# A hand-ordered attention and MLP kernel, with the order of all its tasks and loads written anew

## The chip, the cores and the metric

The kernel runs on one core of a Trainium2 chip. A core has a matrix engine (TensorE; in the profile PE, its weight loads PEld), a vector engine (VectorE, DVE), a scalar engine (ScalarE, ACT), a general engine (GpSimd, POOL) and SyncE (SP), which here only issues DMAs. Each engine works through its own instructions strictly in order and waits on semaphores for the others. The metric is the device time of one execution in microseconds.

## The reference, cut to what matters

Block-sparse attention over 4 batches, 8 heads, 768 positions and 64 columns a head, and behind it a mixing block with weights 768 x 768, 512 x 2048 and 2048 x 512:

```python
scores = q @ k.T / 8                     # per batch and head
mask = near blocks | first/last block row and column | 3 sampled blocks per block row
x = softmax(where(mask, scores, -1e9)) @ v
tok = einsum('ts,bsd->btd', w_tok, alpha1 * x + beta1)
u = x + lam * tok
out = u + lam * (relu((alpha2 * u + beta2) @ w_ch1) @ w_ch2)
```

## The kernel before, in words

The kernel has a fixed prologue and then one long list of words, `ORDER`. A loop reads the list from its first word to its last, and each word emits one task. Since every engine works in order, the list fixes the order of the tasks on each engine; a word also names a PSUM bank (`q0:0`) or an engine (`hq1:d` is VectorE, `:a` ScalarE) where there is a choice. Nothing else schedules the work.

Heads go in 16 pairs p (four a batch). The words, in the order in which a pair needs them:

- `lq`, `lk`, `lv` p: GpSimd issues the load of a pair's q, k or v. Six tiles take turns for these, so a load waits until an earlier tile has been cast. `lt`, `lc`, `lw`, `lx` load the weights and vectors in the same way.
- `cq`, `ck`, `cv` p: a cast or copy of what was loaded, on ScalarE or VectorE. `cq0` is the second head of the first pair, whose data come with the prologue.
- `H` h: TensorE transposes a head of the first five pairs; `hq` and `hk` copy the halves into the operands `qx` and `kx` (four of each, taken in turn). From the sixth pair on a DMA transposes (`tq`, `tk`).
- `hm0` copies the mask rows of `qx[0]` to `qx[1]`. Rows 64 to 87 of `qx` and `kx` carry the block mask in the first five pairs, so a score matmul reads them too. For `qx[2]` and `qx[3]` the prologue copies them by DMA on SyncE (line 401).
- `q` n: the scores of unit n (nine units of 1024 columns a pair), into two PSUM banks; `e` n: the exponential on ScalarE; `m` n: the mask on VectorE, from the sixth pair on; `p`, `r` n: scores times values; `n`, `nt`: the division.
- `M0` makes from the mask rows of `qx[3]` the mask for the later pairs, on VectorE; `N0` and `O0` send it through memory by DMA.
- `W`, `w`: the transposes of the token weights and their copies; `a`, `b`, `k`, `x`, `u`, `U`, `v`: the token mixing and the transposes behind it.
- `f`, `g`: the first channel matmul of batches 0 and 1 and its eviction with ReLU (`g` of the first 16 also copies a column `b1t`). For batches 2 and 3 `y` is a pair of matmuls in a scheme with seven products for eight, `d` its eviction (on ScalarE into a snapshot, or an addition on VectorE), `D` the ReLU. `P`, `S`, `T`, `V`, `Y`, `A` prepare operands on VectorE.
- `h`, `o`: the second channel matmul and its additions; `s`: the store.
- `z480`: a filler, a matmul of 480 columns that no one reads. `F`: a one-element write by VectorE behind which a later load is held.

The lines that the text speaks of:

```python
    for j in range(2, NQB):
        nc.sync.dma_start(qx[j][MB, :], qx[0][MB, :])          # lines 400, 401
    @on("M")
    def _(_i):
        nc.vector.tensor_scalar(
            out=rows[MB, :], in0=qx[3][MB, :], scalar1=-1.0, scalar2=F16MAX, op0=ALU.is_ge, op1=ALU.mult
        )                                                      # line 532
    for word in ORDER.split():
        ...
        step[kind](int(n), *args)
```

Of the kernel before, what the change touches and what calls it, by code (L numbers as in the profile page):

```python
# [54 lines left out]
ck3:d q25:1 F22 w0:d lk5 p12 w5:d e25 p13 q19:3 n2 W4:4 e19 H6:0 F28 lx3 w4:d q22:1 hk6:d r13:1
q17:2 e22 L1 q20:3 hq6:d e17 q24:1 L0 r14 H7:0 e20 q18:2 ck4:d a0 lv3 r15 e18 r16 r17 lc5 b0 q23:3
e24 cv2:d k1:4 n3 lk6 e23 lx1 q21:1 cq4:d r22:1 F42 x1 H9:5 e21 lv6 q28:3 F38 a1 p18:4 lw0 e28 r23
F40 q26:1 b1 p19 e26 hk9:d p20 r24 p21 hq7:d r25 cq6:a q27:3 cv4:d hq9:d r26 lq7 e27 p22 q30:1 hk7:d
k0:5 lw3 n5 e30 lc4 L2 H8:0 F23 F32 x0 q35:3 lw1 hk8:a hq8:d q31:1 lw2 k3:5 n4 e35 lx2 cv3:d q29:0
ck5:a x3 lq5 q32:3 ck6:d e31 k2:4 lk7 a2 e29 lx0 b2 p27:5 q34:1 x2 lv7 p28 u0:d e34 p29 p30 u3:d p31  # L60
lq8 r31:4 q33:0 e32 F37 n6 k4:2 e33 q39:3 x4 r32 u2:a F29 r33 e39 r34 r35 q37:0 n7 q38:1 U1:5 F25
ah6 e38 q40:3 ah7 k5:4 cv6:d e37 bh7 lk8 bh6 q36:1 cq7:d e40 x5 k7:0 lv5 F33 u4:d e36 B0 k6:1 x7
u1:a M0 p36:0 v1:a F39 u5:d p37 p38 x6 q41:1 u6:d U0:1 e41 q43:2 u7:d U2:6 S6 p39 e43 U3:7 v0:d
q44:1 v2:a v3:d p40 q42:2 F26 S7 r40:1 r41 e44 f0:6 f6:7 e42 f3:2 g0:a f5:3 cq5:d g3:d f1:6 tq5 lq11
g5:a F31 n8 r42 f8:2 N0 r43 g8:d f17:0 tk5 f24:3 r44 g24:d f9:2 tk6 S1 f11:3 g9:a g1:d f15:4 ck7:a
S4 f25:2 g11:a n9 f19:5 F30 S3 f12:1 S2 f2:3 g12:a S0 f31:6 g19:a S5 g15:a f26:1 T0 g2:a f10:4 f4:3
g10:a T1 f28:5 g26:a f20:4 g31:a T2 g25:a f16:1 ck8:a f7:2 a4 g4:a f23:6 g17:a T3 O0 f13:3 g7:a tq7
g28:a f18:0 cq8:d cv5:d g13:a f22:5 cv7:d tq6 g16:d g6:a f21:2 g23:d g22:a f27:1 g18:a tk8 P3:d
g20:a g21:d f14:3 g27:a P2:d f29:2 tk7 g14:a F34 b4 lk11 f30:0 g29:d lk9 tq8 cq11:d q53:2 g30:a
q48:1 P4:d k9:1 e53 lk12 A8 A0 lv8 e48 q50:3 q46:2 x9 h0:0 lq10 e46 A9 A1 h14:1 e50 A4 q52:1 o0  # L70
q49:2 e52 q45:3 A2 h1 A10 e49 h2 o12 A11 e45 h15 m48 P0:a F27 m50 lq9 q51:1 q47:2 m49 p48:6 e47 k8:7
F43 m45 m46 e51 p49 p50 o1 q58:2 x8 q56:1 e58 nt16 h16 m51 e56 m52 q60:2 q59:3 h3 o13 e60 A3 p45:2
m58 e59 p46 h17 m53 u8:a m47 u9:a q57:2 q55:3 F36 o2 e57 p47 U4 o14 p51:3 m59 h4 ck11:a m56 p52 e55
p53 nt15 lk14 q63:2 nt17 h18 e63 o3 q64:1 m57 q54:3 e64 q71:2 m60 h5 o15 e54 p57:2 a5 p58 h6 e71 b5
p59 ck12:a m64 q70:2 q62:3 nt19 e70 h19 lk10 m71 e62 q69:1 m54 q61:2 h20 F47 A5 ck9:a m55 p54:6
cq9:a k11:7 lv11 o16 e61 o4 tq9 lq13 h7:1 x11 cq10:a m62 k10:0 tk9 e69 m61 lv9 p60:7 A6 q67:2 tq10
m69 p55 e67 p56 o6 q80:1 x10 p61 e80 p62 nt18 q66:2 h8 nt20 e66 m70 q78:1 ck10:a q68:3 a6 p69:0 e68
p70 lk13 h9 m66 b6 e78 p71 o7 q65:2 q76:3 m63 u10:a q75:1 e65 nt23 h10 m67 u11:a p63:0 cv8:d k12:4
e76 m65 U5 lq12 m68 p66:5 e75 p64 x12 p67 tk10 p68 o8 q81:3 nt22 q86:1 e81 p65 h11 nt21 e86 m75
q74:2 q73:3 a7 e74 k13:0 b7 e73 q72:1 x13 q77:2 o9 u12:a k14:0 u13:a m76 e72 U6 k15:6 x14 A7 e77  # L80
p75:0 p76 x15 q79:1 u14:a m72 q85:2 u15:a h12 m77 e79 U7 m73 p77 e85 q82:3 m80 q93:1 s5 h13 m78 e93
tq11 m79 p78:4 p72:5 m74 e82 p73 p79 tk11 o10 p80 p74 q84:1 P1:d q87:3 nt24 e84 s0 f37:1 m86 tk12
f35:5 e87 nt26 f39:2 ck13:d g35:a m84 lq14 f54:3 g37:a nt25 g39:a q89:2 cv9:d q95:3 e89 q94:0 g54:d
lv10 f38:2 m82 e95 f32:3 P5:d P7:d f34:4 g32:a P6:d f48:5 e94 ck14:d m85 lk15 p84:3 a8 g34:a q83:3
q98:0 e83 p85 cq12:d f47:4 F44 F41 cv11:d tq12 lv15 m81 e98 p86 f61:6 g47:d lv12 g48:a p81:7 m83
q92:0 g61:a q88:2 b8 g38:a p82 f49:6 nt28 e92 m98 f36:2 e88 g49:d f63:3 m89 g36:a q106:0 m87 q91:2
g63:a p83 f51:6 e106 nt27 f56:2 m88 g51:a p87:3 cq13:d e91 f41:7 V0 m94 p88 g56:a q90:0 q96:2 cv10:d
g41:a m93 f52:2 e90 m92 p89 f57:6 m95 g52:a f53:7 e96 V2 p93:2 nt29 g57:a q97:0 q99:2 cq14:d e97
f33:3 m96 tq14 m91 p94 e99 p95 k16:6 m97 tk13 g33:a nt31 g53:a q104:0 m90 q102:1 s2 e104 q103:2 x16
f62:7 s1 a9 e102 tq13 p90:6 p91 p96:0 m99 p92 g62:a p97 nt30 tk14 p98 e103 f60:1 nt32 q113:1 m104  # L90
g60:a q100:2 s3 q105:3 e113 m102 s4 f59:0 b9 k17:1 e100 m113 F45 m103 lq15 e105 f55:2 x17 f44:3 lv14
g59:a m100 g55:a q108:2 m106 q107:0 lv13 e108 q101:3 m105 k18:2 a10 e107 p102:4 f50:5 m108 e101 x18
p99:0 p100 b10 g50:a f58:1 m101 g44:a p103 g58:a q131:3 m107 q115:1 p105:5 A20 e115 f45:1 A12 p106
e131 p104 A16 p101 p107 nt33 g45:a q112:1 k21:6 nt34 e112 nt35 q116:0 A21 q111:1 e116 q130:2 a11
k19:7 e111 x21 h35:0 x19 e130 m111 f43:1 m131 k20:2 g43:a A17 cv12:a o30 q109:2 V4 q114:3 e109 f40:1
A22 f42:3 m112 g40:a f46:4 e114 x20 m109 p111:1 h36 g46:a m114 g42:a cq15:d q110:2 m116 q133:1 e110
q126:3 b11 h37 m115 u16:a p112 ck15:a p113 p114:4 nt37 p115 e126 p116 tk15 p108:5 m130 p109 h28:1
e133 o31 A13 tq15 h38 cv14:a nt38 o24 u20:a q129:1 m110 q127:3 h29 A18 e127 A23 p110 e129 h30 nt36
o32 u21:a q134:2 A19 q132:1 e134 q128:3 o25 h39 m126 u17:a m129 q117:2 e128 U8 h31 m133 u18:a o33
p129:6 u19:a p130 m128 p131 e117 U9 k23:7 a12 e132 h40 o26 U10 nt43 cv15:a h41 x23 b12 u23:a q138:1  # L100
m127 q118:2 q119:3 e118 o34 h32 V5 cv13:a h21:0 m132 e119 m134 k25:4 o27 e138 k24:5 A14 x25 q142:1
o18 q143:3 A15 p126:4 p127 e143 x24 h33 m118 e142 p132:5 m117 h34 m138 p133 o28 p134 q141:1 nt44
q139:3 e141 p117:1 m143 p128 p118 h22 e139 nt42 m119 q135:1 a14 q125:2 e135 k22:6 b14 u24:a p119
e125 x22 h23 m141 u22:a q120:1 nt39 q140:2 e120 q137:3 U11 m142 k29:1 o19 e140 V1 k28:2 m125 u25:a
x29 e137 p141:3 U12 p142 m120 p143 h24 u29:a m139 m140 q123:2 q121:3 o20 e123 p138:1 x28 p139 h25
# [6 lines left out]
d125 p123:0 D124:a p124 a15 D132:a p125 y156 d135:a y163 b15 d147:a y155:1 y148:3 nt41 d142:a y149
d158 y137 y145:0 d151 d148:a k31:1 d145 d162:a V7 d155:a y144 a13 y138:3 d136:a y150 d143:a y157
d138 y164 y146 b13 d149:a y152:2 x31 D158:a y139 D137:d k26:5 u31:a d146 D144:a D145:d d152 d156:a
y159:0 d139 k27:1 d163:a D165:d D151:a x26 D123:a y166:3 x27 y151 y153 d166 u27:a k30:1 D138:d u26:a
d153 D166:a U13 d159 y167 D139:a D125:d y165 D152:a d167 y160 h42:5 D118:d D167:a D131:d d160 D153:a
# [962 lines left out]
```

## Time and profile before

| | us |
|---|---|
| median of three runs | 292.22 (292.13 to 292.43) |
| the profiled execution | 291.82 |
| its span, first to last instruction | 290.1 |
| TensorE busy | 283.9 |
| VectorE busy | 263.8 |
| ScalarE busy | 234.0 |
| GpSimd busy | 53.3 |

The span is the profile's time axis: every start in a row is counted from its first instruction. The profiled execution's own time is 1.7 us longer than its span. A row of a timeline gives start, length, engine, line and operation, output and inputs, how many instructions were merged into it and, in brackets, how long the engine had stood idle before and for whom it waited.

### The profile page before, as it was taken

The numbers are of one execution on the slowest core, as the hardware profiler recorded it, in microseconds if no ns is written. First come the engines' busy times: TensorE is split into PE (matmuls) and PEld (weight loads), VectorE is DVE, ScalarE is ACT, GpSimd is POOL, SyncE is SP. The second block draws the span as 40 slices with busy tenths as digits, with TensorE's granted clock in tenths as the row PEclk, the third lists the DMA queues.
The fourth block names the chain that finished last, engine by engine and source line by source line (L and its number), as shares of the span: only waits on it lengthen the run. The fifth ranks groups of instructions, "written<-read, shape, count | busy, mean of one in ns | idle before, by whom it ended". The sixth has DMA issues, their size and how long they took to land.

```text
span 290.1 us, 8529 instructions
## 1 busy us (share of the span) xinstructions
PE 283.9 (98%) x3538; PEld 213.6 (74%) x3538; DVE 263.8 (91%) x595; ACT 234.0 (81%) x350; POOL 53.3 (18%) x102
## 2 busy tenths in 40 slices
PE   8899999999999999999999999999999999999995
...
GB/s 161 189 246 210 195 211 194 203 165 176 168 115 30 53 140 118 74 164 135 27 186 146 7 2 57 85 3 47 37 75 0 19 112 0 148 145 1 2 42 177
DMA packets 47927, 30.95 MB, mean 107 GB/s; under 512 B 28792, under 2 KB 43984, under 8 KB 47888
## 3 DMA queue, kind: packets, MB, share of 16 engines
...
q14 instruction: 11, 0.09, 0.1%
HBM read 31.16 MB, written 6.88 MB: 131 GB/s over the span
## 4 chain that ended last, share of the span: by engine, by line
PE 87%; ACT 5%; DMA 4%; DVE 2%; issue 1%; POOL 0%; ACTq 0%
PE psum L907 26%; PE psum L997 13%; PE psum L828 12%; PE psum L661 11%; PE psum L763 11%; PE psum L634 9%; PE psum L624 4%; DMA wtk<-in_moe_w_tok_dram 3%; ACT hts L842 2%; ACT eT L645 2%; DMA k2f<-in_k_dram 1%; PE psum L806 1%; PE psum L355 1%; DVE a1p L733 0%; ACT rel L419 0%
## 5 line engine op out<-in xcount | busy, mean ns | idle before, releaser
L645 ACT ACTIVATE eT<-psum 128x1024 f16<-128x1024 f32 (+1 forms) x145 | 140.4, 1028 | 9.3 <-PE psum L634 5.4
L655 DVE TENSOR_TENSOR eT<-eT,maskT 128x960 f16<-128x960 f16 x99 | 61.2, 650 | 0.0
L907 PEld LDWEIGHTS <-hts 128*128 128x128 bf16 x480 | 45.1, 98 | 8.5 <-issue 2.1
L661 PEld LDWEIGHTS <-eT 128*128 128x128 f16 x1152 | 44.4, 97 | 8.3 <-issue 1.7
L661 PE MATMUL psum<-vext,eT 128*128 128x65 f16 x1152 | 48.5, 193 | 0.0
L828 PE MATMUL psum<-uT,w1b 128*128 128x384 bf16 (+1 forms) x256 | 45.9, 327 | 0.1
L1023 ACT ACTIVATE snap<-psum,b1t 128x384 f32<-128x384 f32 x44 | 23.7, 581 | 17.7 <-PE psum L997 13.4
L763 PE MATMUL psum<-a1p,wtokT 128*128 128x128 bf16 x576 | 36.8, 219 | 0.2 <-DVE x_sb L772 0.2
L763 PEld LDWEIGHTS <-wtokT 128*128 128x128 bf16 x576 | 33.2, 98 | 4.1 <-DVE x_sb L772 0.8
L907 PE MATMUL psum<-w2t,hts 128*128 128x256 bf16 x288 | 35.8, 273 | 0.0
L866 DVE TENSOR_TENSOR x_sb<-x_sb,psum 128x256 f32<-128x256 f32 (+1 forms) x61 | 30.7, 514 | 4.7 <-PE psum L907 4.5
L828 PEld LDWEIGHTS <-w1b 128*128 128x128 bf16 x256 | 23.0, 98 | 16.1 <-ACT b1t L419 0.9
L842 ACT ACTIVATE hts<-psum,b1t 128x384 bf16<-128x384 f32 x53 | 29.2, 602 | 0.9 <-PE psum L828 0.5
L634 PE MATMUL psum<-qx,kx 64*128 64x256 bf16 x396 | 29.8, 272 | 0.0
L866 DVE TENSOR_TENSOR hts<-snap,psum 128x384 bf16<-128x384 f32 x48 | 24.7, 547 | 2.7 <-PE psum L997 2.3
L624 PE MATMUL psum<-qx,kx 88*128 88x512 bf16 (+1 forms) x120 | 25.8, 326 | 1.3 <-ACT eT L645 1.0
L907 PE MATMUL psum<-w2b,ss 128*128 128x256 bf16 x192 | 24.6, 273 | 0.0
L907 PE MATMUL psum<-w2b,hts 128*128 128x256 bf16 x192 | 24.4, 273 | 0.0
L634 PEld LDWEIGHTS <-kx 64*128 64x128 bf16 x396 | 15.2, 94 | 8.4 <-issue 3.5
L907 PEld LDWEIGHTS <-ss 128*128 128x128 bf16 x192 | 18.0, 98 | 3.8 <-issue 0.6
L772 DVE TENSOR_TENSOR x_sb<-x_sb,psum 128x384 f32<-128x384 f32 x32 | 17.4, 546 | 1.0 <-PE psum L763 0.8
L997 PEld LDWEIGHTS <-w1b 128*128 128x128 bf16 x128 | 12.1, 98 | 6.6 <-DVE hts L866 0.3
(103 smaller groups left out, 362.5 us busy)
## 6 DMA issues: line engine op xcount, KB each, us to landing
...
```

The source lines that it names most:

```text
L624: nc.tensor.matmul(t[:, f : f + w], kx[h][0:KC, ts(jt, P)], qx[h][0:KC, c : c + w], start=True, stop=True,)
L634: nc.tensor.matmul(t[:, (2 * a + j) * TH : (2 * a + j + 1) * TH], kx[h][r, ts(2 * g + j, P)], qx[h][r, ts(th, TH)], start=True, stop=True,)
L645: nc.scalar.activation(eTs[n][:, c], t[:, c], AF.Exp, bias=EXPB, scale=SCALE)
L655: nc.vector.tensor_tensor(out=e, in0=e, in1=mask, op=ALU.min)
L661: nc.tensor.matmul(ops[key][:, t * VW : t * VW + D + 1], eTs[n][:, c : c + P], vext[n // NU % NV][:, a, jt, 0 : D + 1], start=(first and z ...
L763: nc.tensor.matmul(t[:, j, :], wtokT[:, s, ts(3 * g + j, P)], a1p[p][:, s, :], start=(s == 0), stop=(s == NT - 1),)
L828: nc.tensor.matmul(hps[i][:, 0:w], w1b[:, dk, ts(f, P)], uT[b][:, dk, hf * HS : hf * HS + w], start=(dk == 0), stop=(dk == 3),)
L842: nc.scalar.activation(hts[kk][:, f, :], t[:, 0:HS], AF.Relu, bias=b1t[:, f : f + 1], scale=1.0)
L866: nc.vector.tensor_tensor(out=out, in0=in0, in1=in1, op=op)
L907: nc.tensor.matmul(cps[b, q][:, side * HD : (side + 1) * HD], lhs[:, nk, :], rhs[:, nk, :], start=(z in (0, 6) and nk == 0), stop=(nk == H ...
L997: nc.tensor.matmul(chains[key], lhs[:, dk, ts(f, P)], rhs[:, dk, :], start=(z in (0, 1, 5) and dk == 0), stop=(dk == 1), skip_group_check= ...
L1023: nc.scalar.activation(dst, t, act, bias=bias, scale=1.0)
```

## The change

The list has the same 1589 words before and after: no task is added or taken away. Their order is new from the second word on, and so are many of the PSUM banks; 72 tasks of seven kinds change the engine: of the ReLUs `D` 16 go to ScalarE and 12 to VectorE, of the evictions `g` 8 and 10, of `d` 3 and 4, of the copies `cv` 5 and 1, of `cq` 3 and 2, of `ck` 1 and 3, of `u` 2 and 2. The rest of the file is as it was, two lines further down. The first lines of the list, with the words in the prologue's wake:

```diff
 ORDER = """
-lv0 lk1 lq1 q0:0 lt1 q3:1 cq0 e0 lq2 q2:2 H1:6 lk2 e2 hq1:d q1:0 lv1 z480:7 hm0 z480:7 e1 hk1:d
-cv0:d q5:2 ck1:d e3 lq3 q4:0 p0:6 lt0 e4 p1 p2 lt2 q6:1 cq1:d e5 p3 lk3 p4 H2:7 H3:0 lc2 e6 hk2:d
-q7:2 lc0 F35 W2:1 hq2:d e7 lc1 q8:1 hq3:d r4:7 lk4 r5 w2:d e8 q9:2 cq2:d r6 F24 ck2:d lv2 r7 e9 n0
-z480:1 q12:1 lq6 hk3:d r8 e12 q11:2 n1 W3:6 q10:0 e11 w3:d H5:7 cv1:d q16:1 hk5:d e10 lq4 H4:6 hk4:d
+lv0 lq1 lk1 lt1 lk2 q0:0 q3:1 lq2 cq0 e0 z480:4 M0 lt2 H1:4 q1:3 e3 hq1:d lt0 q2:0 hk1:d lc0 e1
+lv1 hm0 cv0:d q6:1 e2 lc1 q4:2 cq1:d F22 lc2 p0:6 e4 q7:0 lv2 p1 ck1:d p2 e6 lk3 q5:2 p3 lq3 H2:7
+e7 z480:2 hq2:d H3:2 p4 e5 hk2:d q8:0 W2:3 n0 e8 r4:7 q9:2 F27 w2:d r5 W3:6 e9 hk3:d q10:0 hq3:d
+r6 e10 r7 q11:2 ck2:d cq2:d lq4 r8 w3:d e11 q14:1 n1 H4:0 lv3 W4:1 e14 hq4:d q13:2 lw1 W5:6 hk4:d
...
```

Two pieces from the part of batches 2 and 3, the one before and the one after, to show how `y`, `d` and `D` stand:

```diff
-d113:a V6 y121 s10 d127:a p135:0 y115 Y11 d120:a y133:5 d116 d114:a y129 d123 y122 d133:a y117:4
+y135 d113:a d116 y128 d134:a d123 y121 y115 V3 d120:a y136 y138:0 Y11 d135:a y122 d130 y140:2
...
```

In the old list `M0` stands between `B0 k6:1 x7 u1:a` and `p36:0`, some 280 words in; in the new one it is the twelfth word.

More of the change, by code (lines that the diff above doesn't have):

```diff
@@ L49 @@
 ORDER = """
-lv0 lk1 lq1 q0:0 lt1 q3:1 cq0 e0 lq2 q2:2 H1:6 lk2 e2 hq1:d q1:0 lv1 z480:7 hm0 z480:7 e1 hk1:d
-cv0:d q5:2 ck1:d e3 lq3 q4:0 p0:6 lt0 e4 p1 p2 lt2 q6:1 cq1:d e5 p3 lk3 p4 H2:7 H3:0 lc2 e6 hk2:d
-q7:2 lc0 F35 W2:1 hq2:d e7 lc1 q8:1 hq3:d r4:7 lk4 r5 w2:d e8 q9:2 cq2:d r6 F24 ck2:d lv2 r7 e9 n0
-z480:1 q12:1 lq6 hk3:d r8 e12 q11:2 n1 W3:6 q10:0 e11 w3:d H5:7 cv1:d q16:1 hk5:d e10 lq4 H4:6 hk4:d
-W1:4 e16 q15:0 hq5:d p9:5 e15 p10 hq4:d q13:1 F21 cq3:d W0:7 F46 w1:d e13 lv4 q14:0 p11 W5:4 e14
@@ L55 @@
[L55 to L105, printed above, removed]
@@ L106 @@
-nt47 e121 Y8 p140 o21 u28:a q124:1 q122:2 e124 q136:3 nt46 U14 h26 Y9 e122 V3 y112:1 p120:2 m121
-y126:3 e136 y113:4 Y10 h27 d126:a m135 d112:a m122 y127:5 y119:6 o22 y114 d119:a y120:7 d130 s6 y128
-d113:a V6 y121 s10 d127:a p135:0 y115 Y11 d120:a y133:5 d116 d114:a y129 d123 y122 d133:a y117:4
-m136 D116:a p121 y116 d128:a d117 p122 y131:7 d121:a nt40 p136 y118 d131 y130 y140:2 m124 d129:a
-y123 m137 y135 d115:a y132 d118 d140:a y124:3 d132 p137 d122:a y141:1 d124 D117:a y142 y161:4 d144
-d141:a y162:6 m123 y125 d161:a y134:1 nt45 d134:a y143 d165 y154:7 D130:a y136 d137 d154:a y147:6
@@ L112 @@
[L112 to L116, printed above, removed]
@@ L117 @@
-x30 y158 D146:a h49:0 D160:d D159:a o36 d157:a A24 h56:1 u30:a o42 d150:a U15 A28 y175:7 d164:a h43
-A29 s7 y168:4 A25 y189:6 s11 A30 h50 d189:a A32 h51 A26 y217:2 o48 h44 o43 d217:a A33 d175:a h57 Y12
-o37 A34 h52 Y13 h45 d168:d o44 h58 y190:3 o49 h53 o38 Y14 h59 A31 A35 y170 h46 o50 o45 y177 A27 h60
-y191 o51 h54 d190:a o39 s16:w d176:a h55 d193 s9 Y15 s15 h47 o46 d169:d y218:3 y176:0 d221 y192 h61
-d179 d191:a h62 y171 y193 d170:a y169:0 y194:3 d172 h48 o52 D172:a d192:a y173:0 s14 d194 y203:1
@@ L122 @@
-y178 o40 s8 y219 d177:a D193:d y172 s12:w d203:d y204:5 d171:a y182:6 d173 y195 D194:d d218:a y179
-d207 y174 d195 d182:a y180:4 D221:d y205 D173:a d180 y183:3 d204:a y184 D207:d d174 y196:5 d183:a
-y181 d186 y197:0 D174:a d181 y206 d178:a y185 d196:d d205:a y210:3 y208:4 d200 d184:a y187:7 d208
-d210:a y211:0 y198 d187 y220 D208:d d197:a y212 d214 y209 D181:d d211:a y188 d209 y199 d219:a y222:0
-D214:d D179:a d188 y213 d198:a y215:4 D180:d d222 y201:7 d212:a y207 D186:d d201 D188:a y223 D209:a
@@ L127 @@
-y200 d215 y186 D195:a d223 y202 D222:a D200:d y216 D187:d D201:a h77:0 d216 D215:a d202 D223:a y214
-D216:a h70:4 D202:d o66 A36 y221 A44 h63:7 d220:a A37 d206:a h78 d213:a o54 A38 d199:a h64 A40
-d185:a h65 o60 A41 h71 o55 A42 h66 A45 h72 A46 h79 o61 A39 h73 o67 h80 o62 o56 h74 o68 h67 o63 A43
-h81 s22 o57 h75 o69 s21 A47 h76 s23:a h82 o64 h68 s19:a o70 s20 h69 h83 o58 s18 o71 s24:a
+lv0 lq1 lk1 lt1 lk2 q0:0 q3:1 lq2 cq0 e0 z480:4 M0 lt2 H1:4 q1:3 e3 hq1:d lt0 q2:0 hk1:d lc0 e1
+lv1 hm0 cv0:d q6:1 e2 lc1 q4:2 cq1:d F22 lc2 p0:6 e4 q7:0 lv2 p1 ck1:d p2 e6 lk3 q5:2 p3 lq3 H2:7
@@ new lines @@
+e7 z480:2 hq2:d H3:2 p4 e5 hk2:d q8:0 W2:3 n0 e8 r4:7 q9:2 F27 w2:d r5 W3:6 e9 hk3:d q10:0 hq3:d
+r6 e10 r7 q11:2 ck2:d cq2:d lq4 r8 w3:d e11 q14:1 n1 H4:0 lv3 W4:1 e14 hq4:d q13:2 lw1 W5:6 hk4:d
+lc4 e13 H5:7 w4:d q15:1 lw3 hq5:d W0:0 e15 q12:2 w5:d z480:1 W1:1 hk5:d e12 q17:1 lx3 cv1:d q18:3
+w0:d e17 p9:4 lk4 w1:d p10 r13:5 L0 p11 e18 q16:0 F30 L1 p12 p13 e16 q25:1 a0 q23:3 r14 e25 n2 r15
+q19:0 ck3:d e23 r16 F24 b0 q22:1 lv4 cq3:d r17 e19 k0:4 lc5 n3 lk5 e22 F47 F38 q26:3 x0 q24:0 lx2
+a1 e26 H7:4 q20:1 cv2:d H6:5 e24 hq7:d lk6 p18:6 r22:7 r23 hk6:d p19 e20 lw2 q21:0 hk7:d r24 e21
@@ new lines @@
+hq6:d r25 q34:1 b1 q32:2 cv3:d r26 e32 p20 lv6 n5 k1:0 e34 p21 x1 p22 q30:2 F23 F21 u1:d q35:0 e30
+k2:7 cq4:d L2 lq5 n4 e35 q28:1 a2 q29:2 e28 q27:0 F42 F29 x2 k3:6 e29 ck4:d b2 lq6 q31:1 e27 F37
+x3 H8:7 lw0 H9:4 hq8:d e31 k4:5 u2:d hk8:a u3:d p27:6 q33:0 F44 F25 hq9:d ck5:a p28 r31:7 F34 x4
+p29 p30 e33 hk9:d q37:1 lq7 p31 F36 F39 u0:d r32 e37 q42:2 lx1 n6 r33 r34 B0 e42 r35 ah6 q36:0 F28
+n7 U0:6 ck6:a q38:1 u4:d U1:7 e36 bh6 lv5 k5:4 ah7 lx0 e38 bh7 cv4:d q40:0 x5 lk8 k7:5 e40 v0:d
+cv6:d k6:4 v1:a x7 lq8 u5:a q41:0 x6 u7:a q43:1 cq6:d e41 p36:4 cq5:d lv7 r40:5 u6:d p37 tq5 U2:6
@@ new lines @@
+e43 F31 S7 r41 lk7 U3:7 q39:0 v2:a N0 v3:d p38 q44:1 tk5 f2:6 e44 f3:7 e39 tk6 r42 f10:2 g2:a S3
+r43 r44 g3:a f6:3 S6 cq7:a p39 g6:d f15:0 cv5:a lq9 n9 f0:1 g10:d f8:3 lq10 g0:d f13:5 g8:a S4 p40
+f18:1 g15:a S1 f5:2 g18:a S0 f22:3 F46 F33 S2 f17:0 g5:d f1:1 S5 f11:2 T0 f7:6 g11:a f26:7 F26
+g22:a T1 f19:2 g26:a f21:3 ck7:d g1:a T2 f24:7 g21:a f16:1 g7:a F35 F32 F41 n8 cv7:a f20:3 a4 f4:4
+g19:a O0 g13:d f9:6 tq7 g4:a T3 f23:2 g9:a tq6 f30:4 P0:a F43 P2:d f14:5 ck8:d b4 tk8 g16:a f25:6
+F40 g17:d lk13 g23:a f12:1 g24:d g14:a lk10 tk7 P3:d f28:0 g30:a P1:d f31:2 lk9 g25:d g12:a cq8:d
@@ new lines @@
+f27:7 g20:a g31:d tq8 lv8 f29:1 g28:a g27:d h0:6 g29:a P4:d A0 q45:0 q49:1 e45 q52:2 A8 h14:7 A4
+e52 k8:0 A9 cq9:a o12 A10 q48:2 e49 h15 lk11 o0 x8 e48 k9:1 A1 A5 u8:a q51:1 A2 q53:2 e51 h1 x9
+m48 e53 q50:0 m52 h2 e50 m49 q47:1 m51 q46:2 u9:a p48:0 tq9 A3 e46 p49 p51:1 p52 o1 h16 m45 e47 U4
+m50 q58:2 q60:1 m53 e58 h3 A11 e60 o13 q59:2 m58 p50 p53 e59 o2 q57:1 nt17 h17 e57 cq10:d nt16 h4
+lk12 ck10:a o14 m47 q56:0 q54:1 lv9 m46 e56 q55:2 h18 o3 e54 m57 p45:0 p46 m59 p47 e55 q63:1 nt15
+p57:1 p58 e63 m54 p59 q61:2 nt19 h5 e61 m55 q68:0 a5 q71:1 e68 q70:2 h6 b5 e70 o15 p54:0 p55 m56
@@ new lines @@
+k11:1 e71 m61 o4 ck11:a q65:2 q62:1 m68 p56 e65 k10:6 lq11 x11 m60 e62 h19 nt18 ck9:a x10 q69:1
+q67:0 m63 e69 q66:2 tk9 lq12 h7:6 m62 e67 m69 p60:2 tq10 p61 m65 h20 e66 o6 m70 p62 s5 u11:a h8 A6
+cv8:a m66 q75:0 u10:a q64:2 lq14 e75 nt20 h9 U5 o16 e64 p63:2 F45 p66:3 o7 s3 p69:7 m67 q78:0
+q73:2 m71 e78 p70 h10 m64 cv9:a a6 p64 p67 e73 p68 lv15 b6 p71 p65 nt22 q86:0 q76:2 o8 e86 k13:3
+nt23 nt21 e76 q80:0 x13 k12:7 e80 a7 q72:1 b7 q79:2 e72 q85:0 m80 h11 x12 e79 A7 k15:2 o9 u12:a
+k14:3 u13:a m78 e85 U6 x15 p78:7 x14 u15:a q74:2 q77:0 m72 u14:a q84:1 h12 e84 m79 U7 m76 p79 e74
@@ new lines @@
+p80 m73 q82:1 tk10 h13 m75 e77 m74 p75:4 e82 p72:5 o10 p76 p73 m77 s1 q89:0 cq11:a q87:1 m84 p74
+e89 p77 tq11 lv10 nt24 f38:6 P7:d e87 f48:5 nt25 s4 f55:0 P5:d g48:a tk11 P6:d g38:a q83:1 m82
+q81:2 g55:a f51:1 m89 e81 f34:0 m86 f62:6 cq12:d g34:a nt26 lk14 f54:4 g51:a m81 e83 f60:5 ck13:d
+g54:d lq13 f52:7 g60:a ck12:d g62:d tk12 lv11 q91:0 g52:a q88:1 m85 q93:2 e91 p84:6 cq14:d f36:7
+tq12 a8 lv13 e88 p85 p81:0 m83 p86 s2 e93 f57:1 nt28 p82 m91 g57:a q96:1 q95:2 b8 g36:a f61:6 m87
+e95 f53:1 m88 cv10:a f49:7 g53:a p83 lq15 g49:d p87:4 e96 p88 p89 nt27 f42:5 nt29 g61:a q92:0
@@ new lines @@
+g42:a a9 q97:1 q94:3 e97 k16:4 V4 e94 ck14:d f39:5 m97 lk15 f50:2 e92 cq13:d b9 lv12 k17:3 x16
+g39:a m93 g50:a q90:0 x17 q100:2 e90 q102:3 m95 f58:2 m94 e100 f37:3 m90 p93:0 g37:a m92 p94 p95
+e102 f56:1 nt31 p90:3 m96 g56:a p91 p92 g58:a cv11:d q98:2 m100 q105:0 lv14 e98 tq14 q106:3 V0
+k19:2 nt30 e105 tk13 f47:4 m98 e106 x19 p96:5 p97 p98 tq13 g47:a q107:0 m106 q101:1 e107 q99:3
+nt32 f63:4 tk14 cv12:d e99 f41:5 m102 a10 f59:0 s0 g63:a e101 f32:1 m99 k18:4 m107 g59:a b10 g32:a
+q103:1 g41:a x18 q111:3 q104:0 A20 e111 f33:4 m105 k21:5 e104 A16 m101 p105:6 e103 f35:7 m111 p106
```

38 lines of the change are left out of this document (added).

## The prediction

> **What bounds the kernel now.** I read the page first. Its busy times, its slices and the chain that ended last say one thing:
>
> ```profile
> span 290.1 us, 8529 instructions
> PE 283.9 (98%) x3538; PEld 213.6 (74%) x3538; DVE 263.8 (91%) x595; ACT 234.0 (81%) x350; POOL 53.3 (18%) x102
> PE   8899999999999999999999999999999999999995
> PE 87%; ACT 5%; DMA 4%; DVE 2%; issue 1%; POOL 0%; ACTq 0%
> ```
>
> TensorE is busy for 283.9 of 290.1 us and carries 87% of the chain. Where are the other 6.2? Busy times by stretch answer (columns: stretch, length, busy time and instructions of PE, weight loads, VectorE, ScalarE, GpSimd; then granted clock, DMA share, GB/s):
>
> ```profile
> 5.80:8.60 2.80, 2.77 (x19) 1.46 (x19) 1.94 (x6) 2.21 (x4) 2.19 (x4) 1.00 1.11 148
> 8.60:9.40 0.80, 0.02 (x1) 0.03 (x1) 0.76 (x3) 0.80 (x2) 0.00 (x0) 1.00 1.39 178
> 9.40:31.00 21.60, 21.04 (x305) 15.74 (x306) 18.41 (x49) 21.26 (x24) 12.23 (x19) 1.00 1.21 220
> 31.00:287.00 256.00, 255.68 (x3191) 194.28 (x3189) 239.44 (x525) 206.88 (x318) 34.26 (x64) 1.00 0.55 95
> ```
>
> From 31 to 287 us TensorE idles 0.32 us in all. From 9.4 to 31 it idles 0.56, and in one hole, 8.6 to 9.4, 0.78. Both orders hold the same words, so the same matmuls: a new order can win at most about 1.7 us, and every idle microsecond that it adds to TensorE is paid in full. So I looked for what the new order makes TensorE wait for, first where it idles already. The timeline there (start, length, engine, line, operation):
>
> ```profile
> 6.37 0.36 DVE L350 CAST rel<-q2f 128x384 bf16<-128x384 f32 x1
> 6.65 0.35 DVE L350 CAST rel<-k2f 128x384 bf16<-128x384 f32 x1
> 7.28 0.50 PE L355 MATMUL psum<-identb,rel 128*128 128x128 bf16 x6
> 7.81 0.55 DVE L421 COPY qx<-psum 64x768 bf16<-64x768 bf16 x1 [0.81 <-PE psum L355]
> 8.05 0.57 PE L315 MATMUL psum<-warm 128*128 128x480 bf16 x2
> 8.38 0.35 DVE L587 COPY qx<-qx 24x768 bf16<-24x768 bf16 x1
> 8.74 0.56 DVE L421 COPY kx<-psum 64x768 bf16<-64x768 bf16 x1
> 9.33 0.36 DVE L421 COPY vext<-v 128x768 f16<-128x768 f16 x1
> 9.40 1.02 PE L624 MATMUL psum<-qx,kx 88*128 88x256 bf16 x5 [0.79 <-ACT eT L645]
> ```
>
> This is the second head's start-up: casts, transposes (`H1`), VectorE's `hq1`, `hm0`, `hk1` (7.81, 8.38, 8.74 to 9.30), and at 9.40 the first scores that need that head. The profile names ScalarE as the releaser; the copy that ended at 9.30 is an operand of this matmul, so I take VectorE.
>
> **The change: `M0`, the term that decides.** `M0` (line 532) moves from the 283rd word to the 12th, and on VectorE from 49.2 us (row below) to the place right behind the casts of 6.37 to 7.00, ahead of `hq1`. It reads the mask rows of `qx[3]`, which line 401 copies there by DMA, and VectorE works in order. So: when does that copy land? Nothing of before waits for it early; its landing is not in the profile and has to be bounded. SyncE's issues, `M0` by its tile (duration, start), and what each DMA queue moved in 9.2 to 9.9, in 9.9 to 13.0 (twice: packets, then size is 0.07 MB), in 12.7 to 13.0 and in 13.0 to 16.0:
>
> ```profile
> 3.05 1.59 SPq L290 DMA_DIRECT2D kx<-ind_c  x4
> 5.31 2.11 SPq L401 DMA_DIRECT2D qx<-qx  x2
> 56.10 1.32 SPq L593 DMA_TRANSPOSE qx<-rel  x1
> ```
> ```profile
> L532 DVE TENSOR_SCALAR maskT<-qx x1: 351/351/351, 49.2 to 49.2; 24x768 f16<-24x768 bf16 x1
> ```
> ```profile
> q0 software_dynamic: 103, 0.12, 105.1%
> ```
> ```profile
> q0 software_dynamic: 466, 0.57, 105.7%
> q1 hardware_dynamic: 72, 0.07, 8.5%
> ```
> ```profile
> q0 software_dynamic: 80, 0.06, 124.1%
> q1 hardware_dynamic: 3, 0.00, 2.3%
> ```
> ```profile
> q0 software_dynamic: 764, 0.61, 129.7%
> q8 instruction: 1, 0.02, 1.9%
> ```
>
> After line 401 SyncE issues nothing until 56.10, so what its queue (q1) moves in 9.9 to 13.0 is line 401's: 0.07 MB are its two copies of 36 KB. They were issued at 5.31, but none of their packets goes in 9.2 to 9.9, the last go in 12.7 to 13.0, and none in 13.0 to 16.0: GpSimd's loads (q0) hold the engines. The second copy is the one for `qx[3]`. I take its landing at 13.3 (0.3 for the last packet and its signal); bounds 12.7 and, since the new order issues GpSimd's loads more densely, 14.5.
>
> A rule speaks against that. The Trainium skill ("DMA: Bandwidth & Descriptors", section on queues, rings and completion order) says that each DMA engine takes turns between the queues that have work, a packet at a time. By that two small copies beside one busy queue should be through soon after their issue. The trace has them 4.6 us after it and more, so this rule alone does not time them; what it would give is the third rival.
>
> Then, with the lengths of the rows: landing 13.3, `M0` starts at 13.33 and takes 0.35; `hq1` to its successor 0.57, `hk1` 0.56, `hm0` 0.36, and 0.10 to the matmul: 15.27 for `q6`, the first score of that head, which stood in the same place as 9.40. TensorE has nothing before it in its order (`q1` and `q2` are done by 8.5). **+5.87 us.** Behind `M0` on VectorE stand also the first value copy `cv0` and the casts of the next pair; GpSimd's `lv2` waits for the slot that `cv0` frees, so it stops until about 15.6. I cost that at nothing: loads already issued still fill the DMA engines, and v2 is the values of the third pair.
>
> **What an idle TensorE costs when it resumes.** It will stand for about 7 us. The only stretch where this trace has it start from rest is the beginning:
>
> ```profile
> 1.26 3.09 PE L315 MATMUL psum<-warm 128*128 128x512 bf16 x12
> 2.09 0.15 PEld L315 LDWEIGHTS <-warm 128*128 128x128 bf16 x1 [0.28 <-issue]
> 2.52 0.15 PEld L315 LDWEIGHTS <-warm 128*128 128x128 bf16 x1 [0.28 <-issue]
> 3.80 0.38 PEld L315 LDWEIGHTS <-warm 128*128 128x128 bf16 x5 [0.28 <-issue]
> 15.38 0.37 PE L315 MATMUL psum<-warm 128*128 128x480 bf16 x1
> ```
>
> 512 columns take 0.43 us there (2.09 to 2.52); later 480 columns take 0.20 (two in 0.57 at 8.05, one in 0.37 at 15.38). So TensorE runs at half pace until 3.80, nearly 3 us from its first matmul, and loses 1.5. No later hole exceeds 0.8 us, so whether 7 us bring the slow start back is not in this trace: bounds 0 and, for a start twice as long, 3. I take the start's own **+1.5**. The Trainium skill ("TensorE: Matmul & The Clock Gate", Part 1) states that the clock falls to half after an idle window of about 3.4 us and returns after one busy window as long; by that estimate the term is 1.7 and the sum 0.2 higher.
>
> **The other edits.** The weights' loads `lt2`, `lt0` come ahead of several others, so the transposes `W` no longer wait for them:
>
> ```profile
> 13.28 0.54 PE L496 MATMUL psum<-identb,wtk 128*128 128x128 bf16 x6 [0.22 <-DMA wtk<-in_moe_w_tok_dram]
> 19.10 0.51 PE L496 MATMUL psum<-identb,wtk 128*128 128x128 bf16 x6 [0.15 <-DMA wtk<-in_moe_w_tok_dram]
> ```
>
> **-0.4**, and with TensorE 6 us later these loads are early in any case. Of the three fillers `z480`, two lie in the old hole and cost nothing; now one does and two stand among work: **+0.2** (the 0.20 above). Tasks change engines, and ScalarE gains most by four ReLUs and four value copies. Its shortest feedback to TensorE is the snapshot eviction between two matmul pairs on one bank:
>
> ```profile
> L1033 ACT ACTIVATE hts<-hts 128x384 bf16<-128x384 bf16 x28 | 13.0, 515 | 0.8 <-DVE hts L866 0.7
> L419 ACT COPY vext<-v 128x768 f16<-128x768 f16 x4 | 3.3, 833 | 0.0
> L1023 ACT ACTIVATE snap<-psum,b1t 128x384 f32<-128x384 f32 x44 | 23.7, 581 | 17.7 <-PE psum L997 13.4 <-DVE hts L866 3.9
> 255.21 12.74 PE psum L997 x78
> ```
>
> Four times 0.515 and four times 0.833 are 5.4 us at most, against 49 us that ScalarE is free in 31 to 287: nothing on the path while that cover lasts, up to 5.4 without it. A word `y` (two matmuls) takes 2 x 12.74 / 78 = 0.33. Counted in the lists, 11 evictions `d` now have only three `y` words between the one they read and the one they hold up (0.98 us), where before had one such place. An eviction needs 0.58 plus about 0.25 of matmul tail and signals, so 0.15 is left, and a ReLU queued ahead (0.515) breaks it: between 0 and 10 x 0.37 = 3.7. The one such place of before lies in a stretch that idles 0.32 in all; I stay near it, **+0.3**. The order of the DMA transposes and of later loads I cost at nothing: before shows no wait of TensorE on either after 31 us, and they are now 6 us ahead.
>
> Sum: 5.87 + 1.5 - 0.4 + 0.2 + 0.3 = +7.5. The profiled execution took 291.82 (span 290.1 and 1.7 around it), which makes 299.3; the median of the three runs shown is 0.4 higher, 292.22, so 299.7.
>
> **The rivals.**
> 1. The wait comes, TensorE does not slow down after it: for it, no row shows a clock falling mid-kernel; against it, the start. 292.2 + 6.0 = 298.2.
> 2. The snapshots' tight places cost their upper bound: 299.7 + 3.4 = 303.1. For it, eleven places with 0.15 to spare; against it, 49 us of free ScalarE.
> 3. Not slower: the copy for `qx[3]` lands before 7.0 and `M0` costs only itself. Then `H1` ends near 7.6 and `q6` starts at about 7.64 + 0.57 + 0.56 + 0.36 + 0.10 = 9.23, 0.17 before the 9.40 of now; with -0.4 and +0.2 that is 291.8. It decides from a landing before about 7.3, 6 us earlier than the packets go; q1's packets speak against it, and only a different mix of loads speaks for it.
>
> **How the numbers follow.** Forecast 0.61, rival 1 0.18, rival 2 0.12, rival 3 0.09. Predicted: 299.7. The range has to leave out rival 3 and part of rival 2: 297.0 (rival 1, a landing at 12.7, no snapshot waits) to 302.0 (landing 14.5 and half as much again for the slow start and some of rival 2). What a measurement can tell from no change is 0.2%, 0.6 us. Rival 3 splits: faster 0.04, same 0.05; slower 0.91.
>
> **What would show it.** In the profile after: VectorE idle from about 7.0 to 13.3, ended by the DMA `qx<-qx`, with line 534's mask operation (now that number) behind it; TensorE's hole from 8.4 to about 15.3; then matmuls at half pace for some 3 us (a granted clock below 1.00 there); no wait at the `W` transposes; 31 us to the end nearly as full as now. If `M0` starts before 8 the forecast is wrong from its first step; if TensorE idles over 1 us after 40 us, the snapshots or another queue cost more than I gave them.

## The result and the profile after

The new list took 298.86 us in the median of six runs (298.00 to 299.54), the old one 292.33 beside it: a ratio of 1.0224, 95% interval 1.0207 to 1.0241. It is 6.5 us slower; 299.7 had been forecast. The profiled execution took 299.54, the longest of the six, with a span of 297.7.

Its page, in the lines that answer to those of before (busy times, TensorE's slices and its granted clock in tenths, the chain):

```profile
span 297.7 us, 8521 instructions
PE 285.8 (96%) x3538; PEld 215.7 (72%) x3538; DVE 263.7 (89%) x593; ACT 236.0 (79%) x352; POOL 53.1 (18%) x102
PE   7289999999999999999999999999999999999995
PEclk9759999999999999999999999999999999999999
PE 93%; DMA 4%; DVE 2%; ACT 1%; issue 0%; ACTq 0%; SPq 0%
```

TensorE's second slice (7.4 to 14.9 us) is busy for only two tenths and its clock is below full in the second and third; the rest looks as before. The timeline of that stretch:

```profile
6.51 1.03 PE L626 MATMUL psum<-qx,kx 88*128 88x512 bf16 x6 [0.34 <-ACT qx L396]
7.38 0.34 DVE L352 CAST rel<-k2f 128x384 bf16<-128x384 f32 x1
8.12 1.03 PE L626 MATMUL psum<-qx,kx 88*128 88x512 bf16 x5
14.04 0.35 DVE L534 TENSOR_SCALAR maskT<-qx 24x768 f16<-24x768 bf16 x1 [6.31 <-DMA qx<-qx]
14.40 0.55 DVE L423 COPY qx<-psum 64x768 bf16<-64x768 bf16 x1
14.96 0.56 DVE L423 COPY kx<-psum 64x768 bf16<-64x768 bf16 x1
15.55 0.35 DVE L589 COPY qx<-qx 24x768 bf16<-24x768 bf16 x1
15.96 1.87 PE L626 MATMUL psum<-qx,kx 88*128 88x512 bf16 x5 [6.80 <-DVE qx L589]
```

VectorE has finished the casts and stands 6.31 us until the DMA `qx<-qx` lands; then come `M0`, `hq1`, `hk1`, `hm0`, and TensorE resumes at 15.96 after 6.80 us. Busy times by stretch (length, PE, weight loads, VectorE, ScalarE, GpSimd, then the granted clock) show what followed, and the rest of the kernel:

```profile
9.20:15.90 6.70, 0.00 (x0) 0.10 (x1) 1.80 (x4) 1.56 (x2) 1.81 (x3) 0.67 1.15 202
11.00:11.40 0.40, 0.00 (x0) 0.00 (x0) 0.00 (x0) 0.00 (x0) 0.40 (x1) 1.00 1.05 213
11.50:12.00 0.50, 0.00 (x0) 0.00 (x0) 0.00 (x0) 0.00 (x0) 0.18 (x2) 0.50 1.05 201
15.96:21.60 5.64, 5.64 (x47) 3.70 (x47) 0.89 (x4) 3.57 (x4) 2.16 (x3) 0.50 1.12 256
21.80:22.20 0.40, 0.40 (x8) 0.29 (x6) 0.28 (x1) 0.11 (x1) 0.00 (x0) 1.00 1.25 243
23.00:31.00 8.00, 8.00 (x116) 6.33 (x115) 7.77 (x20) 7.89 (x9) 3.94 (x6) 1.00 0.67 87
31.00:294.50 263.50, 263.40 (x3323) 200.76 (x3319) 247.49 (x545) 217.50 (x329) 37.50 (x69) 1.00 0.58 96
```

In the middle of the hole, between 11.4 and 11.5, the clock falls to 0.50; it stays there for the first 5.6 us of matmuls. From 15.96 to 31 us TensorE is never idle and from 31 us to the last matmul it idles 0.10 us in all: behind its hole this list is fuller than the old one, which lost 0.56 up to 31 us and 0.32 after.

### The profile page after: what moved, and what is told of

It is laid out like the page before. It is cut to its first block, busy times and chain, and to the rows that moved or that the text cites. A ratio compares the mean times of both kernels' runs of the same rounds, so it can differ in the third digit from the quotient of the medians.

```text
span 297.7 us, 8521 instructions
## 1 busy us (share of the span) xinstructions
PE 285.8 (96%) x3538; PEld 215.7 (72%) x3538; DVE 263.7 (89%) x593; ACT 236.0 (79%) x352; POOL 53.1 (18%) x102
## 4 chain that ended last, share of the span: by engine, by line
PE 93%; DMA 4%; DVE 2%; ACT 1%; issue 0%; ACTq 0%; SPq 0%
PE psum L909 25%; PE psum L830 13%; PE psum L663 12%; PE psum L999 12%; PE psum L765 11%; PE psum L636 9%; PE psum L626 7%; DMA qx<-qx 2%; DMA k2f<-in_k_dram 1%; PE psum L357 1%; PE psum L498 1%; DVE hts L846 1%; PE psum L808 0%; ACTq L281 0%; ACT rel L350 0%
## 5 line engine op out<-in xcount | busy, mean ns | idle before, releaser
L647 ACT ACTIVATE eT<-psum 128x1024 f16<-128x1024 f32 (+1 forms) x145 | 139.2, 1031 | 15.4 <-PE psum L626 9.8
L663 PE MATMUL psum<-vext,eT 128*128 128x65 f16 x1152 | 47.8, 195 | 0.0
L830 PE MATMUL psum<-uT,w1b 128*128 128x384 bf16 (+1 forms) x256 | 45.0, 326 | 0.1
L909 PE MATMUL psum<-w2t,hts 128*128 128x256 bf16 x288 | 35.1, 273 | 0.0
L830 PEld LDWEIGHTS <-w1b 128*128 128x128 bf16 x256 | 23.3, 98 | 16.0 <-issue 0.8
L626 PE MATMUL psum<-qx,kx 88*128 88x512 bf16 (+1 forms) x120 | 26.9, 342 | 7.2 <-DVE qx L589 6.8
L844 ACT ACTIVATE hts<-psum,b1t 128x384 bf16<-128x384 f32 x51 | 28.3, 590 | 1.3 <-PE psum L830 0.5
L626 PEld LDWEIGHTS <-kx 88*128 88x128 bf16 x120 | 10.0, 100 | 11.7 <-issue 7.4
```

The lines of the kernel that those rows point to most:

```text
L626: nc.tensor.matmul(t[:, f : f + w], kx[h][0:KC, ts(jt, P)], qx[h][0:KC, c : c + w], start=True, stop=True,)
L647: nc.scalar.activation(eTs[n][:, c], t[:, c], AF.Exp, bias=EXPB, scale=SCALE)
L663: nc.tensor.matmul(ops[key][:, t * VW : t * VW + D + 1], eTs[n][:, c : c + P], vext[n // NU % NV][:, a, jt, 0 : D + 1], start=(first and z ...
L830: nc.tensor.matmul(hps[i][:, 0:w], w1b[:, dk, ts(f, P)], uT[b][:, dk, hf * HS : hf * HS + w], start=(dk == 0), stop=(dk == 3),)
L844: nc.scalar.activation(hts[kk][:, f, :], t[:, 0:HS], AF.Relu, bias=b1t[:, f : f + 1], scale=1.0)
L909: nc.tensor.matmul(cps[b, q][:, side * HD : (side + 1) * HD], lhs[:, nk, :], rhs[:, nk, :], start=(z in (0, 6) and nk == 0), stop=(nk == H ...
```

## The experiments

My theory: `M0`'s wait and the slow TensorE behind it are the whole change. The rivals: the new order costs time elsewhere; the clock has nothing to do with it; it is the new mix of loads that makes the copy late. Each kernel was compared with the old list run beside it (median 292.33 for the new list, 292.0 to 292.1 for the others; in the last comparison one run, 292.57).

| kernel | median, us | ratio to the old list (95%) |
|---|---|---|
| new list | 298.86 | 1.0224 (1.0207 to 1.0241) |
| new list, `M0` moved back | 292.21 | 1.0019 (1.0000 to 1.0037) |
| old list, `M0` moved forward | 298.67 | 1.0225 (1.0208 to 1.0243) |
| new list, `M0` reads `qx[0]` | 292.79 | 1.0023 (1.0002 to 1.0045) |
| new list, 28 fillers in the hole | 296.20 | 1.0150 (1.0126 to 1.0174) |
| new list, 14 fillers in the hole | 298.06 | 1.0204 (1.0177 to 1.0230) |
| `M0` moved back, `ck7` later | 291.20 | 0.9966 (0.9950 to 0.9982) |
| the same without two fillers | 291.02 | 0.9968 (0.9952 to 0.9984) |
| new list, `kx` copies behind | 298.18 | one run |
| new list, loads held | 298.45 | one run |

### `M0` alone, in both directions

```diff
-lv0 lq1 lk1 lt1 lk2 q0:0 q3:1 lq2 cq0 e0 z480:4 M0 lt2 H1:4
+lv0 lq1 lk1 lt1 lk2 q0:0 q3:1 lq2 cq0 e0 z480:4 lt2 H1:4
...
-u7:a q43:1 cq6:d e41 p36:4
+u7:a q43:1 cq6:d e41 M0 p36:4
```

> The new list with M0 alone moved back to just ahead of p36, where the old list has it. Theory (M0's wait for the copy of the mask rows, and the slow TensorE behind it, is all that the change costs): the hole of 5.9 us and the 2.7 us of half pace go, and up to 1.4 us of early stalls that the hole had hidden may come back: 290.3 to 291.7 us. Rival (the new order costs time in other places too): 294 us or more. No wait for the DMA qx<-qx in the profile either way.

292.21 us: one word moved back takes away 6.65 us and leaves the two lists within 0.4% of each other. The other way round, in the old list:

```diff
-H1:6 lk2 e2 hq1:d
+H1:6 lk2 e2 M0 hq1:d
...
-u1:a M0 p36:0
+u1:a p36:0
```

> The old list with M0 alone moved ahead of hq1, as in the new one. Theory: VectorE waits for the DMA qx<-qx until 13 to 14 us, TensorE resumes near 15.3 to 16 and at half pace, and some of the old list's 1.4 us of stalls between 9.4 and 31 us disappear behind the hole: 299.2 to 300.9 us. Rival (the denser early loads of the new list are what makes the copy late): the copy lands before 9 us here and the time stays below 294 us.

298.67 us, 6.6 above the old list and 0.5 below what I had expected, with the same wait in the timeline and the same fall of the clock by stretch:

```profile
13.12 0.35 DVE L532 TENSOR_SCALAR maskT<-qx 24x768 f16<-24x768 bf16 x1 [6.13 <-DMA qx<-qx]
```
```profile
11.00:12.00 1.00, 0.00 (x0) 0.00 (x0) 0.00 (x0) 0.00 (x0) 0.00 (x0) 1.00 1.07 213
12.10:15.00 2.90, 0.00 (x0) 0.00 (x0) 1.81 (x4) 0.00 (x0) 0.00 (x0) 0.50 1.21 186
15.10:18.80 3.70, 3.70 (x32) 2.39 (x33) 0.80 (x3) 1.82 (x2) 3.13 (x6) 0.50 0.54 78
18.90:20.00 1.10, 1.10 (x27) 1.10 (x25) 0.22 (x1) 0.94 (x2) 1.10 (x3) 1.00 1.07 207
```

So the place of this one word decides in either list, and the new mix of loads is not needed for the wait.

### Is it the DMA or the place on VectorE?

```diff
-            out=rows[MB, :], in0=qx[3][MB, :], scalar1=-1.0, ...
+            out=rows[MB, :], in0=qx[0][MB, :], scalar1=-1.0, ...
```

> The new list with M0 in its early place, reading the mask rows of qx[0], which the prologue writes itself, instead of the copy in qx[3] (the values are the same). Theory (it is the DMA, not the place on VectorE): M0 costs its own 0.35 us ahead of hq1 and nothing else, 290.3 to 292.2 us, within 0.5 us of M0 moved back. Rival (the place in VectorE's order costs by itself): 294 us or more.

292.79 us, 0.6 above the top of what I had expected and 0.6 above the kernel with `M0` moved back, whose interval it overlaps. In its profile `M0` starts at 7.86, right behind the casts and without a wait. With `M0` early and no DMA to wait for, 6.1 of the 6.5 us are gone: the place alone costs little, if anything.

### Is it the clock?

```diff
-lv1 hm0 cv0:d q6:1
+lv1 hm0 cv0:d z480:5 z480:5 (28 in all) z480:5 q6:1
```

> The new list with 28 more fillers of 480 columns (28 x 0.20 = 5.6 us at full pace) just ahead of q6, in a bank that nobody uses then, so that TensorE works through most of the hole. Theory (an idle TensorE comes back at half pace): granted clock 1.00 after the hole, and 2.7 us less than the new list, about 296.2 us. Rival (the slow matmuls behind the hole have another cause, such as late operands): they stay slow and the time stays at 298.9 us.

296.20 us, as expected: 2.7 us for a TensorE that is kept at work while VectorE waits for the copy as before (`M0` starts at 13.29 here, after a wait of 4.93). Timeline and stretches of the profiled execution, the longest of the four (297.69):

```profile
11.03 5.83 PE L317 MATMUL psum<-warm 128*128 128x480 bf16 x28
16.71 1.03 PE L626 MATMUL psum<-qx,kx 88*128 88x512 bf16 x5
```
```profile
10.30:16.70 6.40, 6.40 (x33) 3.12 (x32) 2.72 (x8) 1.94 (x2) 2.66 (x5) 1.00 1.14 210
16.70:22.00 5.30, 5.30 (x76) 4.00 (x75) 1.84 (x6) 4.23 (x5) 1.30 (x2) 1.00 1.14 261
```

The same five matmuls take 1.03 here and 1.87 in the new list. But in this execution the fillers outlast the wait: `hm0` is done at 15.16 (14.81 and 0.35), and TensorE comes to the scores at 16.71. So the 2.7 us are what is left after such an overrun, and the operands were not late here; that part of the rival needs the next run. Half as many fillers:

> The new list with 14 more fillers (2.8 us) at the start of the hole, which leaves TensorE some 4 us without work instead of 6.8. If the clock falls only after an idle stretch as long as one whole window of the 3.4 us that its records show as a unit, wherever it begins, it mostly does not fall here: 296.2 us, as with 28 fillers. If 2 to 3 us without work are enough (in the new list's profile the clock fell 2.3 us after the last matmul), it falls: 297.9 us or more.

298.06 us: the clock fell. My reckoning of the rest of the hole was off, since the fillers began at 10.37 in this execution; what was left was not 4 us but 1.73, and even that was enough:

```profile
10.37 3.00 PE L317 MATMUL psum<-warm 128*128 128x480 bf16 x14
15.10 1.03 PE L626 MATMUL psum<-qx,kx 88*128 88x512 bf16 x5 [1.73 <-DVE qx L589]
```
```profile
15.10:16.40 1.30, 1.30 (x14) 0.83 (x14) 0.89 (x4) 0.24 (x1) 0.67 (x1) 1.00 1.03 201
16.50:19.80 3.30, 3.30 (x36) 2.61 (x35) 0.00 (x0) 3.30 (x4) 1.40 (x2) 0.50 1.14 274
19.90:22.00 2.10, 2.10 (x36) 1.78 (x35) 2.02 (x6) 0.99 (x3) 0.00 (x0) 1.00 1.14 264
```

Here the five matmuls came straight behind the wait for their operands and still took 1.03, so it is not late operands that make them slow. The clock fell 1.3 us after TensorE had resumed and stayed low for 3.4 us. The four runs are of two kinds: 297.26 and 297.39 (the profiled one) with a mean granted clock of 0.993 and 0.994, and 298.74 and 298.80 with 0.989. A mean of 0.994 over 296 us is what 3.4 us at 0.50 give, 0.989 what 6.8 us give, so by this estimate the low stretch lasted twice as long in the other two; how long their TensorE had idled was not seen.

### Why `M0` moved back gives nothing more, and a faster version

The run with `M0` moved back missed its 290.3 to 291.7. Its timeline has a wait that the new list does not have, where the same cast comes some 7 us later (74.08):

```profile
66.62 0.36 DVE L423 COPY rel<-k 128x768 bf16<-128x768 bf16 x1 [0.99 <-DMA k<-in_k_dram]
66.90 1.22 DVE L868 TENSOR_TENSOR w2t<-w2b 128x2048 bf16<-128x2048 bf16 x1
68.34 0.56 DVE L714 TENSOR_TENSOR x_sb<-psum,rcp 128x384 f32<-128x384 f32 x1
68.95 0.83 PE L830 MATMUL psum<-uT,w1b 128*128 128x385 bf16 x4 [0.89 <-DVE x_sb L714]
```

The cast `ck7` waits for its load, and behind it on VectorE stands the division `n8`, whose bank `f4` needs. So:

```diff
-f21:3 ck7:d g1:a T2 f24:7 g21:a f16:1 g7:a F35 F32 F41 n8 cv7:a f20:3
+f21:3 g1:a T2 f24:7 g21:a f16:1 g7:a F35 F32 F41 n8 ck7:d cv7:a f20:3
```

> The new list with M0 moved back and the cast ck7 moved from behind f21 to just behind the division n8. In the run with M0 alone moved back VectorE waits 0.99 us at ck7 for the load of that pair's k, and TensorE 1.05 us at f4 for n8 behind it. Theory (without the hole the new order needs that load earlier than it lands, and nothing else holds f4): that wait goes, 291.2 us, 0.8 under the old list. Rival (another late load or the busy VectorE takes its place): 292.0 to 292.2 us.

291.20 us, as expected, and faster than the old list by 0.2 to 0.5%: two moved words make the new list the better one. In its profile TensorE is busy throughout 66 to 71 us; the wait at `f4` is gone. Then the fillers among work:

```diff
-e7 z480:2 hq2:d
+e7 hq2:d
...
-w5:d z480:1 W1:1
+w5:d W1:1
```

> The kernel with M0 and ck7 moved, without the two fillers z480 that stand among work. If a filler among work costs its 0.20 us and no hole there is long enough to slow TensorE, 0.4 us less than with them: 290.8 us, granted clock 1.00 throughout. Rival (they stand where TensorE waits anyway): the same time as with them.

291.02 us, ratios of 0.9968 and 0.9966: no difference that can be told, but both intervals are wide enough that 0.4 us is not excluded either. So this run decides neither for the expectation nor for the rival. From 8.6 to 31 us TensorE is busy for 21.67 of 22.40 us with them and for 21.59 without, and gets through 335 and 340 matmuls:

```profile
8.60:31.00 22.40, 21.67 (x335) 16.97 (x335) 19.41 (x49) 22.23 (x25) 12.18 (x18) 1.00 1.17 220
```
```profile
8.60:31.00 22.40, 21.59 (x340) 17.08 (x341) 19.39 (x50) 22.30 (x25) 12.34 (x19) 1.00 1.16 218
```

### Why the copy lands so late

```diff
-    for i in (2, 3):
-        for w in range(2):
-            nc.sync.dma_start(kx[i][MB, ts(w, HS)], ind_dr.ap()[:, ts(w, HS)])
...
     for j in range(2, NQB):
         nc.sync.dma_start(qx[j][MB, :], qx[0][MB, :])
+    for i in (2, 3):
+        for w in range(2):
+            nc.sync.dma_start(kx[i][MB, ts(w, HS)], ind_dr.ap()[:, ts(w, HS)])
```

> The new list with the four copies into the mask rows of kx[2] and kx[3] issued behind line 403's copies instead of ahead of them on the same queue. Theory A (SyncE's queue is served in order and slowly beside GpSimd's loads, so what stands ahead of a copy delays it): the copies for qx start about 3.4 us earlier and M0 starts near 10 to 11 us; the time falls by about as much. Theory B (the copies wait for a turn whatever stands ahead of them on their queue): M0 starts at 13 to 14 us as before.

`M0` started at 12.52, neither theory's figure. The copies were issued at 5.40, and what stood ahead of them on SyncE's queue (q1) was through by 6 us: the 0.15 MB that it moved in 10 to 13 us are the size of the two copies and of the four behind them. Yet in 6 to 10 us only GpSimd's queue moved packets:

```profile
q0 software_dynamic: 747, 0.64, 118.3%
```

The other part, GpSimd's loads:

```diff
-lv0 lq1 lk1 lt1 lk2 q0:0 q3:1 lq2 cq0 e0 z480:4 M0 lt2
+lv0 lq1 lk1 q0:0 q3:1 cq0 e0 z480:4 M0 G0 lt1 lk2 lq2 lt2
...
+    @on("G")
+    def _(_i):
+        nc.gpsimd.tensor_copy(out=held[D : D + 1, 0:1], in_=rows[D : D + 1, 0:1])
```

> The new list with GpSimd's loads from the fourth on held until M0 is done (a one-element copy of M0's output on GpSimd ahead of lt1), so that only three loads, 0.58 MB, run beside the copies of line 403. Theory (GpSimd's loads hold the DMA engines; with the order on SyncE's own queue changed the wait only shrank by some 1 us): M0 starts by 10 to 11 us instead of 14.0. Rival (SyncE's queue is slow by itself): 13 to 14 us as before. The total is no measure here, since every weight load comes later.

`M0` started at 11.40, 0.4 later than expected at the latest. In both runs the first scores start earlier than in the new list's profile, so start and wait are both given (timeline of the first, then of the second):

```profile
12.52 0.35 DVE L534 TENSOR_SCALAR maskT<-qx 24x768 f16<-24x768 bf16 x1 [5.46 <-DMA qx<-qx]
```
```profile
11.40 0.35 DVE L534 TENSOR_SCALAR maskT<-qx 24x768 f16<-24x768 bf16 x1 [4.45 <-DMA qx<-qx]
```

What the queues moved in the second of these runs in 6 to 8, in 8 to 10 and in 10 to 12 us:

```profile
q0 software_dynamic: 373, 0.27, 101.7%
q1 hardware_dynamic: 69, 0.04, 8.2%
```
```profile
q0 software_dynamic: 327, 0.23, 77.8%
q1 hardware_dynamic: 66, 0.06, 9.8%
```
```profile
q0 software_dynamic: 19, 0.01, 4.3%
q1 hardware_dynamic: 13, 0.01, 1.8%
```

The 0.07 MB of q1 from 8 us on are the size of the two copies: they go as the three loads run out, and `M0` starts 1.7 us before the earliest start beside all loads. Those starts are 14.04 in the new list, 13.29 and 13.18 with 28 and 14 fillers and 13.12 in the old list with `M0` moved forward. So the loads hold the copies at least in part, and the four `kx` copies ahead do not explain the wait: with them out of the way no packet went before 10 us, and `M0` started only 0.6 us before the earliest of the four. VectorE's wait says no more, since it changes with the start (5.46 us in the first run, 4.45 in the second, but 4.93 to 6.31 in the three runs that leave the new list's loads and copies as they are). Each figure is from one execution. Why a copy with nothing ahead of it on its own queue goes over 4 us without a packet beside the loads stays open.

## Why the prediction was right, and where its sizes were off

**The hole, +5.87.** Right in mechanism and size. The profiled execution as a whole starts later (first scores at 6.51 instead of 5.83, behind a later load), so the times shift. Counted from the first scores, the second head's came 3.57 us later in the old list (9.40 less 5.83), 9.44 in the forecast (15.27 less 5.83) and 9.45 in the new list (15.96 less 6.51). The chain that I took from the old rows, 0.35 + 0.57 + 0.56 + 0.36 + 0.10, is 1.94; it took 1.92 (14.04 to 15.96). That the whole agrees to 0.01 is luck: in the run with 14 fillers, which has the same loads and copies, it was 8.38 (15.10 less 6.72). Nor do the old rows give a length for the 0.3 that I put between the last packet and the landing. In the new list q1's last packet goes at 13.5, and `M0` starts 0.5 later. Taking VectorE's copy rather than ScalarE for the releaser at 9.40 was right too: the profile now names VectorE.

**The slow start behind it, +1.5.** Right in kind, too small: the fillers make it 2.7, and half of the 5.64 us for which the matmuls ran at 0.50 is 2.8. I sized it by the kernel's own beginning, 3 us at half pace; in the profiled execution the half pace lasted 5.6 us, in the old list with `M0` moved forward 3.7. The bounds, 0 and 3, held it. The Trainium skill ("TensorE: Matmul & The Clock Gate", Part 1) says that the monitor looks at free-running windows of 3.4 us. The trace agrees as to the unit: low for 10.2 us in the new list (three windows; from between 11.4 and 11.5 to 21.7), 6.8 in the old list with `M0` moved forward (12.0 to 18.8), 3.4 in the run with 14 fillers (16.4 to 19.8). The page's one idle window of 3.4 us before a fall does not: 1.73 us without work were enough there. In these three traces the clock came back at the end of the first whole unit of 3.4 us that TensorE worked through (counted from the fall: 18.3 to 21.7, 15.4 to 18.8, 16.4 to 19.8). So the half pace lasted until then, and how long that was hung on where in such a unit the work resumed.

**The weights' loads, -0.4, and later loads at nothing.** By my reckoning this is the term that was mis-sized most. No wait at a `W` is left, as said, but the hole hid more than those two: the hole and the clock cost 5.9 + 2.7 = 8.6 us, the new list lost 6.5, so some 2.1 us of other waits went. That figure is rough, since it sets medians against the hole of one execution. Against the old list 0.78 us of it can be read off: behind its hole TensorE idled 0.56 + 0.32 us there and 0.10 here. The run with `M0` moved back shows a wait that the new order has of its own and that the hole hid, 0.89 us at `f4` behind `ck7`; moving `ck7` was worth 1.01 us (292.21 less 291.20). What makes up the rest was not traced. I had costed later loads at nothing because they would be 6 us ahead; that was true of the new list. What the sum lacked was a credit for the waits that the hole would hide, and so the time came out 0.8 too high although the clock's term was 1.2 too low.

**The fillers, +0.2.** Not settled: without the two that stand among work the time fell by 0.18 us in the median, which cannot be told from 0 or from 0.4.

**The snapshots, +0.3.** Not seen. In 214 to 239 us, with the first of the matmul pairs and evictions, the new list's TensorE is busy throughout, and to the last matmul at 294.5 it idles 0.02 us more:

```profile
214.00:239.00 25.00, 25.00 (x262) 17.71 (x260) 24.50 (x54) 23.30 (x49) 0.00 (x0) 1.00 0.10 30
```

So three words between an eviction's source and its successor are enough here, and rival 2 falls. My count of such places was uneven: with exactly three `y` words between, whatever else stands there, the lists have 11 and, before, 5; with three and no other matmul word, 9 and 1. Rival 1 falls by the granted clock, rival 3 by the wait itself; the copy was as late beside the old list's loads (`M0` at 13.12, after a wait of 6.13). The turns a packet at a time between queues, which the Trainium skill states ("DMA: Bandwidth & Descriptors", section on queues, rings and completion order) and from which rival 3 drew, did not time these copies: `M0` started at 14.04.
